# Values with the score as the stationary operand in the first two units, and transposes into x

## The chip, the cores and the metric

The kernel runs on one core of a Trainium2 chip. A core has five engines that work side by side, each through its own queue in the order of the program: TensorE (PE) multiplies matrices, VectorE (DVE) and GpSimd (POOL) do elementwise work, ScalarE (ACT) does functions and copies, and SyncE (SP) issues transfers (DMAs) here. They wait for each other by semaphores. TensorE reads its operands from SBUF, the large on-chip memory of 128 partitions, and writes only into PSUM, a small memory from which VectorE and ScalarE copy results away. GpSimd does not work on PSUM in this kernel. The metric is the time of one execution on the device in microseconds (us).

## The reference, cut to what matters

```python
# r, k, v, w: (4, 8, 768, 48); u: (8, 48)
for t in range(S):
    cur = einsum('bhd,bhe->bhde', u * k[t], v[t])
    y[t] = einsum('bhd,bhde->bhe', r[t], state + cur)
    state = w[t][..., None] * state + einsum('bhd,bhe->bhde', k[t], v[t])
x = y.transpose(0, 2, 1, 3).reshape(B * S, H * D)     # (3072, 384)
h = x @ moe_w_in                                      # (384, 2048)
out = (h / (1 + exp(-h))) @ moe_w_out                 # (2048, 384)
```

An attention with a decaying state, and behind it a network of two matrices with SiLU between them. All inputs and the output are float32.

## The kernel before, in words

**Units.** The work is cut into 12 units, each of 128 tokens (L = 128) of two of the four batches (b = 0 and 1). Of a unit, the attention gives x, 384 channels by 256 tokens; `up` (8 steps of 12 matmuls and a SiLU on ScalarE, L987 and L996) gives h; `down`, or `quarter` in later units, gives the output rows.

**Scores.** Within a unit a token sees the earlier ones through a matrix of scores, 128 keys by 128 queries for each batch and head, with the keys in partitions. The tile `score` holds all of it in two halves: e = 0 the even heads and e = 1 the odd ones; the heads of one half are counted by p = 0 to 3, so head h is 2p + e. Seven levels fill it (`scores`, levels 0 to 6, for blocks of 1 to 64 tokens): matmuls into a bank of PSUM (L704, L712), then per half either a masked copy by VectorE (`keep_masked`, L722) or two to four plain copies of blocks by ScalarE (L741). The list COPIED (L686) names the (unit, level, half) that ScalarE copies. `bonus_write` (L604, VectorE) writes the diagonal part with u; it reads it in unit 0 from p_w, a part of PSUM that the weights use too. Between the levels keys grow by products on GpSimd (L645, L669) and odd ones are copied by ScalarE (L615, L659), and queries grow by products on VectorE (L627).

**y in the first two units.** The units 0 and 1 have no earlier state to add. `y` (L859) takes, for each batch and head, the values as stationary operand (64 columns: the head's 48 and 16 beyond it, which is why the rooms of the values are 16 columns longer and set to zero there) and the scores as moving operand (128 columns). The output has channels in partitions: even heads from 0, odd heads from 64, so two matmuls lie in two halves of the array's columns. ScalarE copies the result of each batch to yt (L869).

**x in the first two units.** The channels of yt stand at 0 and 64, those of x have to stand without gaps. `dense_x` (L897) moves them with six matmuls per batch by matrices of ones, `dense`, which `clear_dense` (GpSimd, L303) and `make_dense` (ten copies by ScalarE, L317) build at the start. Of the four results ScalarE copies three to xt, and VectorE the second of unit 0 (L905). Later units use `y_state`, `y_values` and transfers instead (`move_x`), which the change leaves alone.

**Weights.** The kernel prepares the network's weights itself, while the first units run: 16 pieces, each loaded by a DMA into a staging place (L206, some of them only once an older piece has left the place) and split and joined again: `head_weight` (ScalarE, L223 and L225), `tail_weight` (ScalarE, L231, into p_w), `join_weight` (VectorE, L242 and L243, out of p_w), `add_weight` (GpSimd, L255). p_w holds one piece: L231 of the next waits for L243 of the one before. `up` waits for pieces 0 to 7, `down` for 8 to 15.

**The order** is written out by hand, in lists of steps given to `do` (from L1094); each engine gets its instructions in the order of these lists. Around the change in unit 0:

```python
do((bonus, 1, 0), (bonus, 1, 1), (bonus, 1, 2), *both(y, 0), (turn_apart, 0), (join_weight, 0), (add_weight,),
   (product, 1, 0), (tail_weight, 1), (turn, 1, 0, "k"), (join_weight, 1), (dense_x, 0, 0), (turn, 1, 1, "k"),
   (dense_x, 0, 1), (grow_queries, 1, 0), (odd_ones, 1), (tail_weight, 2), (turn_k, 0), (head_weight, 2), ...
   (up, 0, 0), ...
```

and in unit 1 (L1127): `(scores, 1, 6)`, steps of piece 8 and of unit 2, `(up, 0, 7)`, y, `(turn_apart, 1)`, `(tail_weight, 9)`, `(turn_k, 1)`, dense_x of b = 0, the first half of `head_weight` 9, dense_x of b = 1, its second half, `join_weight` 9, `tail_weight` 10, `head_weight` 10, `update` (L879 and L895), `(up, 1, 0)`. `turn_apart` (L820) is 16 small matmul records on TensorE and `turn_k` (L828) two copies of their results on ScalarE; `turn` of k is two copies for each b (L394, L395). `beat` (L1088) are transposes without use of their result.

Of the kernel before, what the change touches and what calls it, by code (L numbers as in the profile page):

```python
# [8 lines left out]
F32 = mybir.dt.float32  # L9
# [29 lines left out]
def kernel(  # L39
# [11 lines left out]
    nc = tc.nc  # L51
# [32 lines left out]
    def bank(name, *dims):  # L84

        have = banks[name][turns_of[name] % 2][:]
        turns_of[name] += 1
        steps, n = [], 1
        for d in dims[::-1]:
            steps.insert(0, [n, d])  # L90
            n *= d
        return bass.AP(tensor=have.tensor, offset=have.offset, ap=[have.ap[0], *steps])
# [33 lines left out]
    def load_values(i):  # L126
        n, b0 = units[i]
        t0 = n * L

        rooms = [pin.tile([128, H * D + PD - D], F32, name=name, bufs=2) for name in ("vt", "vq")]  # L130
        if n == 0:
            for room in rooms:
                nc.vector.memset(room[:, H * D:], 0.0)
        whole[i] = rooms
        vt[i], vq[i] = (room[:, 0:H * D].rearrange("p (h d) -> p h d", h=H) for room in rooms)
        nc.sync.dma_start(out=vt[i], in_=v[b0, :, t0:t0 + L, :].rearrange("h t d -> t h d"))
        if i < NTOK:
            nc.sync.dma_start(out=vq[i], in_=v[b0 + 1, :, t0:t0 + L, :].rearrange("h t d -> t h d"))
            return

        for g in range(4):
            t1 = t0 + L - (g + 1) * 32
            nc.sync.dma_start(out=vq[i][g * 32:(g + 1) * 32], in_=v[b0 + 1, :, t1:t1 + 32, :].rearrange("h t d -> t h d"))
# [152 lines left out]

    parts = sorted({(ch // 128, ch // (2 * D)) for ch in range(DM)})
    assert len(parts) == KC * 2

    dense = pt.tile([128, H, 2, D], F32, name="ruk", bufs=1).rearrange("p h s d -> p (h s d)").rearrange("p (x t) -> p x t", t=128)  # L300

    def clear_dense():
        nc.gpsimd.memset(dense, 0.0)  # L303

# [5 lines left out]

    def make_dense():
        for x, (c, p) in enumerate(parts):
            for e in range(2):
                at, rows = (2 * p + e) * D, slice(PD * e, PD * e + D)
                d0, d1 = max(0, c * 128 - at), min(D, (c + 1) * 128 - at)
                if d0 < d1:
                    nc.scalar.copy(out=dense[rows, x, at + d0 - c * 128:at + d1 - c * 128],  # L317
                                   in_=ident[rows, PD * e + d0:PD * e + d1])

# [366 lines left out]
    COPIED = (0, 5, 0), (0, 6, 0), (1, 6, 0)  # L686
# [172 lines left out]
    def y(i, b):  # L859

        p_yt[i, b] = ps.tile([128, NP, L], F32, name="p_h", bufs=2) if i == 0 else bank("p_m", NP, L)
        for p in range(NP):
            for e in range(2):
                h = 2 * p + e
                nc.tensor.matmul(p_yt[i, b][PD * e:PD * e + PD, p, :], lhsT=whole[i][b][:, h * D:h * D + PD],
                                 rhs=score[:, i % NSC, e, b * NP + p, :], start=(p == 0), stop=(p == NP - 1))
        if b == 0:
            yt[i] = pt.tile([128, NP, NB, L], F32, name="yt", bufs=1)
        nc.scalar.copy(out=yt[i][:, :, b, :], in_=p_yt[i, b])  # L869
# [27 lines left out]
    def dense_x(i, b):  # L897

        if b == 0:
            xt[i] = pt.tile([128, KC, TU], F32, name="xt", bufs=1)  # L900
        p_x = ps.tile([128, KC, L], F32, name="p_h", bufs=2) if i == 0 else bank("p_m", KC, L)
        for x, (c, p) in enumerate(parts):
            nc.tensor.matmul(p_x[:, c, :], lhsT=dense[:, x, :], rhs=yt[i][:, p, b, :],
                             start=(x == 0), stop=(x == len(parts) - 1))
        (nc.vector.tensor_copy if (i, b) == (0, 1) else nc.scalar.copy)(out=xt[i][:, :, b * L:(b + 1) * L], in_=p_x)  # L905
# [174 lines left out]
    def do(*steps):  # L1080
        for fn, *args in steps:
            fn(*args)
# [7 lines left out]
    def back(fn, i, *args):  # L1090
        return both(fn, i, *args)[::-1]
# [3 lines left out]
       (bonus_sum, 0, 0), (clear_dense,), (clear_state,), *back(turn, 0, "w"), (bonus, 0, 2), (bonus_sum, 0, 1), (start_keys, 0, nc.vector, True),  # L1095
       (start_keys, 0, nc.vector, False), (grow_queries, 0, 0), (product, 0, 0, nc.vector), (odd_keys, 0, 1), (grow_keys, 0, 1),
       (make_dense,), (beat, 16))
# [5 lines left out]
    for l in range(1, NL):  # L1103
        do((scores, 0, l), *[(grow_keys, 0, l + 1)] * (l + 1 < NL), *others[l])

    do((bonus, 1, 0), (bonus, 1, 1), (bonus, 1, 2), *both(y, 0), (turn_apart, 0), (join_weight, 0), (add_weight,),
       (product, 1, 0), (tail_weight, 1), (turn, 1, 0, "k"), (join_weight, 1), (dense_x, 0, 0), (turn, 1, 1, "k"),
       (dense_x, 0, 1), (grow_queries, 1, 0), (odd_ones, 1), (tail_weight, 2), (turn_k, 0), (head_weight, 2),
# [13 lines left out]
    for m in range(1, 4):  # L1122
# [4 lines left out]
    do((scores, 1, NL - 1), (bonus, 2, 0), (bonus, 2, 1), (join_weight, 8), (add_weight,), (bonus_sum, 2, 0), (bonus, 2, 2), (up, 0, 7), *both(y, 1), (turn_apart, 1),  # L1127
       (tail_weight, 9), (turn_k, 1), (dense_x, 1, 0), (head_weight, 9, [0]), (dense_x, 1, 1), (head_weight, 9, [1]),
# [66 lines left out]
```

## Time and profile before

| | |
|---|---|
| median of 3 runs | 606.24 us (606.04 to 606.5) |
| the profiled execution | 607.39 us, of which the span of the profile is 605.6 |
| granted clock of TensorE | 1.0 |
| busy in 30 to 66 us (36 us) | TensorE 34.1, VectorE 31.6, ScalarE 31.6, GpSimd 30.4 |
| busy in 66 to 90 us (24 us) | TensorE 23.5, VectorE 18.6, ScalarE 19.3, GpSimd 18.7 |
| y of unit 0 and unit 1 on TensorE | from 29.41 and from 66.75 |
| x of unit 0 and unit 1 on TensorE | from 32.51 and from 69.27 |

In a line of the profile, L12 is line 12 of the kernel before. PE is a matmul, PEld a load of its stationary operand; a float32 matmul shows as two records of each, so that 16 matmuls are "x32". A line of the timeline begins with the start and the length in us; lengths of matmuls overlap, so the pace is the distance from start to start. Names such as p_h<-score,vt are the tile written and the tiles read. A bracket at the end of a line is the time in which the engine stood idle before it, and who ended that. A line of waits names the waiting and the awaited group, then the sum in us, the number of waits and the longest. The chain is followed backwards from the last instruction, at each step to what released it.

### The profile page before, as it was taken

The page shows a single profiled execution, that of the slowest core. Times are in us where ns is not written, and L with a number is a line of the kernel's source. Part 1 is how long each engine was busy: PE and PEld are TensorE (multiplying, and loading weights), DVE is VectorE, ACT ScalarE, POOL GpSimd, SP SyncE. Part 2 cuts the span into 40 slices and gives each one's busy share as a digit, 9 for nine tenths or more (in the row PEclk, how much of TensorE's full clock was granted, in tenths as well). Part 3 has the DMA queues.
Part 4 walks back from the last instruction along what each step waited for, and adds up shares of the span by engine and source line. Part 5 has one row for each costly group of instructions (what it writes and reads, how often), then busy time and mean ns, then how long its engine had stood idle before and what let it go on. Part 6 is the DMA issues. An engine that isn't in the chain of part 4 may idle for free.

```text
span 605.6 us, 15147 instructions
## 1 busy us (share of the span) xinstructions
PE 593.4 (98%) x5982; PEld 529.5 (87%) x5982; DVE 416.8 (69%) x709; ACT 233.2 (39%) x516; POOL 366.6 (61%) x414
## 2 busy tenths in 40 slices
PE   8999999999998999999999999999999999999997
PEld 7787876799888899888889889889889989989997
DVE  7879779798795695696696687587587587451041
ACT  6788874431520530440351351351252242241110
POOL 6998777357578578378478478478568558500000
PEclk9999999999999999999999999999999999999999
DMA  9966693343532543643642643543553441100000
GB/s 224 312 148 168 124 307 47 56 77 49 127 70 48 106 65 52 137 61 56 130 65 50 130 62 53 121 69 52 115 83 53 98 70 27 36 2 27 28 1 26
DMA packets 203079, 53.44 MB, mean 88 GB/s; under 512 B 186752, under 2 KB 194816, under 8 KB 203008
## 3 DMA queue, kind: packets, MB, share of 16 engines
q1 hardware_dynamic: 201424, 51.88, 42.0%
q8 instruction: 47, 0.77, 0.6%
q10 hardware_dynamic: 1584, 0.59, 0.5%
q14 instruction: 24, 0.20, 0.1%
HBM read 43.21 MB, written 5.24 MB: 80 GB/s over the span
## 4 chain that ended last, share of the span: by engine, by line
PE 75%; DVE 8%; DMA 5%; POOL 3%; ACT 3%; SPq 2%; issue 2%; DVEq 0%; POOLq 0%; ACTq 0%
PE p_h L987 31%; PE p_o L1053 31%; PE p_m L1009 3%; PE p_m L852 2%; PE p_sc L704 2%; DMA tokens_w<-in_w_dram 2%; POOL tk L645 2%; DVE temps L1035 2%; PE p_m L704 1%; SPq L123 1%; PE p_m L844 1%; DVE score L722 1%; DVE tr L627 1%; DMA u_bc<-in_u_dram 1%; DVE p_w L242 1%
## 5 line engine op out<-in xcount | busy, mean ns | idle before, releaser
L987 PE MATMUL p_h<-xt,w_in_sb 128*128 128x256 f32 x1152 | 259.0, 382 | 0.9 <-POOL tk L669 0.7
L987 PEld LDWEIGHTS p_h<-xt,w_in_sb 128*128 128x128 f32 x1152 | 215.8, 190 | 32.1 <-POOL tk L669 0.9
L996 ACT ACTIVATE gt<-p_h 128x512 f32<-128x512 f32 x90 | 53.6, 597 | 189.4 <-PE p_h L987 189.1
L645 POOL TENSOR_TENSOR tk<-tk,tw 128x256 f32<-128x256 f32 x128 | 91.2, 734 | 42.8 <-issue 22.9
L1053 PE MATMUL p_o<-own,temps 128*128 128x192 f32 x528 | 88.7, 327 | 3.8 <-DVE temps L1062 3.8
L1053 PEld LDWEIGHTS p_o<-own,temps 128*128 128x128 f32 x528 | 86.0, 190 | 4.7 <-DVE temps L1062 4.6
L1053 PE MATMUL p_o<-w_out_sb,gt 128*128 128x192 f32 x508 | 87.4, 328 | 0.0
L1053 PEld LDWEIGHTS p_o<-w_out_sb,gt 128*128 128x128 f32 x508 | 82.7, 190 | 0.9 <-issue 0.4
L507 POOL TENSOR_TENSOR ruk<-tokens_rk 128x768 f32<-128x768 f32 (+1 forms) x32 | 51.3, 1613 | 49.6 <-DMA tokens_rk<-in_k_dram 25.5
L1035 DVE TENSOR_TENSOR temps<-gt 128x256 f32<-128x256 f32 x84 | 55.8, 664 | 22.4 <-ACT gt L996 22.4
L627 DVE TENSOR_TENSOR tr<-tr,tw 128x512 f32<-128x512 f32 x61 | 56.4, 925 | 18.2 <-PE p_m L704 14.4
L422 POOL TENSOR_TENSOR tw<-tw 128x256 f32<-128x256 f32 (+6 forms) x83 | 43.1, 519 | 37.1 <-DVE tw L374 33.2
L615 ACT COPY tk<-tk 128x256 f32<-128x256 f32 x52 | 21.0, 404 | 97.0 <-POOL tk L645 70.1
L1062 DVE TENSOR_TENSOR partial<-p_o,partial 128x192 f32<-128x192 f32 x33 | 11.8, 358 | 38.3 <-PE p_o L1053 38.1
L722 DVE COPY_PREDICATED score<-mask,p_sc 128x512 f32<-128x512 int8 x42 | 31.2, 798 | 3.1 <-PE p_sc L704 2.9
L1035 DVE TENSOR_TENSOR temps<-temps,gt 128x256 f32<-128x256 f32 x43 | 32.2, 748 | 1.5
L1053 PE MATMUL p_o<-w_out_sb,temps 128*128 128x192 f32 x176 | 30.4, 326 | 0.0
L1062 DVE TENSOR_TENSOR temps<-p_o,partial 128x192 f32<-128x192 f32 x22 | 7.9, 357 | 32.7 <-PE p_o L1053 23.3
L507 POOL TENSOR_TENSOR spare<-tokens_rk 128x384 f32<-128x384 f32 (+1 forms) x16 | 29.3, 1833 | 0.0
L857 ACT COPY yt<-p_m 48x512 f32<-48x512 f32 x40 | 23.2, 581 | 14.9 <-PE p_m L852 10.1
L1053 PEld LDWEIGHTS p_o<-w_out_sb,temps 128*128 128x128 f32 x176 | 28.9, 190 | 0.0
L704 PEld LDWEIGHTS p_sc<-tr,tk 48*32 48x32 f32 (+1 forms) x1312 | 18.2, 119 | 11.3 <-issue 6.8
(187 smaller groups left out, 840.5 us busy)
## 6 DMA issues: line engine op xcount, KB each, us to landing
w_out_sb<-in_moe_w_in_dram SPq DMA_DIRECT2D x6, 768.0 KB, 7.4
w_out_sb<-in_moe_w_out_dram SPq DMA_DIRECT2D x4, 768.0 KB, 5.8
own<-in_moe_w_out_dram SPq DMA_DIRECT2D x4, 768.0 KB, 6.2
tokens_rk<-in_r_dram SPq DMA_DIRECT2D x8, 384.0 KB, 4.4
tokens_rk<-in_k_dram SPq DMA_DIRECT2D x8, 384.0 KB, 5.4
tokens_w<-in_w_dram SPq DMA_DIRECT2D x8, 384.0 KB, 6.4
xt<-yt SPq DMA_DIRECT2D x60, 48.0 KB, 2.0
raw<-in_w_dram SPq DMA_DIRECT2D x80, 32.0 KB, 2.0
```

Source lines behind the costliest of these rows:

```text
L422: engine.tensor_tensor(out=up, in0=t[:, :, 0::2], in1=t[:, :, 1::2], op=ALU.mult)
L507: mul = lambda out, one, two: nc.gpsimd.tensor_tensor(out=out, in0=one, in1=two, op=ALU.mult)
L615: nc.scalar.copy(out=keys(i, X[(l + 1) % 2] * L + c, [4 * c, blocks], [c, 2], [1, c]), in_=keys(i, NP * L + c, [4 * c, blocks], [NP * L + ...
L627: nc.vector.tensor_tensor(out=odd, in0=odd, in1=tw[i][l][:, :, 0::2][:, :, :, None].to_broadcast([128, Q, L >> (l + 1), c]), op=ALU.mult)
L645: nc.gpsimd.tensor_tensor(out=out, in0=have, in1=odd_products(i, l, b, *blocks), op=ALU.mult)
L704: nc.tensor.matmul(to, lhsT=tk[i][rows, X[l % 2] + p, x * m:(x + 1) * m], rhs=have, start=True, stop=True)
L722: nc.vector.copy_predicated(out=dst, mask=masks[l][:, :, None].to_broadcast([128, NB, NP, ni, c]), data=sc[e].rearrange("p (b q) (i c) -> ...
L857: nc.scalar.copy(out=yt[i][PD * e:PD * e + D, :, b, :], in_=p_yt[i, e][PD * b:PD * b + D])
L987: nc.tensor.matmul(p_h[:, a, :], lhsT=w_in_sb[:, c, f * 128:(f + 1) * 128], rhs=xt[i][:, c, :], start=(c == 0), stop=(c == KC - 1))
L996: nc.scalar.activation(out=gt[i, m], in_=p_h, func=AF.Silu)
L1035: nc.vector.tensor_tensor(out=out, in0=one, in1=two, op=op)
L1053: nc.tensor.matmul(p, lhsT=left(f), rhs=right[:, f, :], start=(f == 0), stop=(f == FH - 1))
```

## The change

In units 0 and 1, `y` takes the scores as stationary operand (128 columns) and the values as moving operand (48 columns). The output has tokens in partitions and the 384 channels side by side without gaps, one bank for each batch. The matmuls go through both batches of the half e = 0 first, then of e = 1; one ScalarE copy of 384 columns per batch follows. `turn_x` then makes x by three transposes of 128x128 for each batch. The matrix of ones, its making and clearing, and the 16 zero columns of the values go. COPIED has one entry more: ScalarE, not VectorE, copies half e = 1 of the last level of unit 0. The steps keep their places in the lists, but for the two calls of y that become one.

```diff
-        rooms = [pin.tile([128, H * D + PD - D], F32, name=name, bufs=2) for name in ("vt", "vq")]
-        if n == 0:
-            for room in rooms:
-                nc.vector.memset(room[:, H * D:], 0.0)
+        rooms = [pin.tile([128, H * D], F32, name=name, bufs=2) for name in ("vt", "vq")]
...
-    def clear_dense():
-        nc.gpsimd.memset(dense, 0.0)
-    def make_dense():
...
-    COPIED = (0, 5, 0), (0, 6, 0), (1, 6, 0)
+    COPIED = (0, 5, 0), (0, 6, 0), (0, 6, 1), (1, 6, 0)
...
-    def y(i, b):
-        p_yt[i, b] = ps.tile([128, NP, L], F32, name="p_h", bufs=2) if i == 0 else bank("p_m", NP, L)
-        for p in range(NP):
-            for e in range(2):
-                h = 2 * p + e
-                nc.tensor.matmul(p_yt[i, b][PD * e:PD * e + PD, p, :], lhsT=whole[i][b][:, h * D:h * D + PD],
-                                 rhs=score[:, i % NSC, e, b * NP + p, :], start=(p == 0), stop=(p == NP - 1))
-        if b == 0:
-            yt[i] = pt.tile([128, NP, NB, L], F32, name="yt", bufs=1)
-        nc.scalar.copy(out=yt[i][:, :, b, :], in_=p_yt[i, b])
+    def y(i):
+        p_y = [ps.tile([128, H * D], F32, name="p_h", bufs=2) if i == 0 else bank("p_m", H * D) for b in range(NB)]
+        for e in range(2):
+            for b in range(NB):
+                for p in range(NP):
+                    h = 2 * p + e
+                    nc.tensor.matmul(p_y[b][:, h * D:(h + 1) * D], lhsT=score[:, i % NSC, e, b * NP + p, :], rhs=values(i, b)[:, h, :],
+                                     start=(e == 0 and p == 0), stop=(e == 1 and p == NP - 1))
+        yt[i] = pt.tile([128, NP, NB, L], F32, name="yt", bufs=1)
+        for b in range(NB):
+            y_rows[i, b] = yt[i].rearrange("p q b t -> p (q b t)")[:, b * H * D:(b + 1) * H * D]
+            nc.scalar.copy(out=y_rows[i, b], in_=p_y[b])
...
-    def dense_x(i, b):
+    def turn_x(i, b):
...
-        for x, (c, p) in enumerate(parts):
-            nc.tensor.matmul(p_x[:, c, :], lhsT=dense[:, x, :], rhs=yt[i][:, p, b, :],
-                             start=(x == 0), stop=(x == len(parts) - 1))
+        for c in range(KC):
+            nc.tensor.transpose(p_x[:, c, :], y_rows[i, b][:, c * 128:(c + 1) * 128], ident)
         (nc.vector.tensor_copy if (i, b) == (0, 1) else nc.scalar.copy)(out=xt[i][:, :, b * L:(b + 1) * L], in_=p_x)
```

## The prediction

> **What bounds the kernel now.** I read the page first, for shares of busy time and the chain.
>
> ```profile
> PE 593.4 (98%) x5982; PEld 529.5 (87%) x5982; DVE 416.8 (69%) x709; ACT 233.2 (39%) x516; POOL 366.6 (61%) x414
> PE 75%; DVE 8%; DMA 5%; POOL 3%; ACT 3%; SPq 2%; issue 2%; DVEq 0%; POOLq 0%; ACTq 0%
> ```
>
> TensorE is the bound of the whole, but a quarter of the chain runs elsewhere. The waits of TensorE from 90 us on show that little of that is late:
>
> ```profile
> PE p_o L1053 <- DVE temps L1062: 3.8, 2, 2.4
> ```
>
> These two waits hang by their chains on scores that TensorE itself finished, so they move with it. A shift of TensorE at 90 us therefore reaches the end whole, and the change lies wholly before 90. There I took the chain in order of time:
>
> ```profile
> 29.99 1.96 PE p_h L865 x30
> 31.95 0.63 PE p_sc L820 x16
> 32.58 1.55 PE p_h L903 x12
> 34.15 0.48 ACT xt L905
> ...
> 39.81 0.78 ACT p_w L231
> 40.61 0.97 DVE p_w L242
> ...
> 63.96 2.86 PE p_h L987 x12
> ```
>
> The reader is to see that unit 0's y and x (L865, L903) stand on the chain, and that after them it runs not through the matmuls of up but through the rounding of weights (ScalarE L231, VectorE L242, GpSimd L255), which feeds `up` at 63.96. In the timeline ScalarE is gapless from 34.15 to L231 at 39.71, and VectorE from L242 at 40.61 to 60.37. So what is late on ScalarE at 34.15 is late on TensorE at 63.96. Last, the timeline at both places of the change:
>
> ```profile
> 31.99 0.59 ACT L869 COPY yt<-p_h 128x512 f32<-128x512 f32 x1 [0.29 <-PE p_h L865]
> 32.47 0.88 ACT L231 ACTIVATE p_w<-w_out_sb 128x768 f32<-128x768 uint16 x1
> 34.15 0.48 ACT L905 COPY xt<-p_h 128x384 f32<-128x384 f32 x1 [0.19 <-PE p_h L903]
> ...
> 68.76 0.59 ACT L869 COPY yt<-p_m 128x512 f32<-128x512 f32 x1 [0.28 <-PE p_m L865]
> 69.25 0.89 ACT L231 ACTIVATE p_w<-w_out_sb 128x768 f32<-128x768 uint16 x1
> 72.26 0.48 ACT L905 COPY xt<-p_m 128x384 f32<-128x384 f32 x1
> 73.00 5.45 PE L987 MATMUL p_h<-xt,w_in_sb 128*128 128x256 f32 x24
> ...
> 89.34 0.70 PE L704 MATMUL p_sc<-tr,tk 48*64 48x64 f32 x32 [0.55 <-POOL tk L669]
> ```
>
> Right behind each second copy of y stands L231, the tail of the next weight: that is what y delays. 0.55 us is the only slack of TensorE between 72 and 121.
>
> [...] here are the loads.
>
> ```profile
> 25.07 0.97 PEld L590 LDWEIGHTS p_w<-own_sums,partial 128*128 128x128 f32 x8
> 32.51 2.75 PEld L903 LDWEIGHTS p_h<-yt,ruk 128*128 128x128 f32 x24
> 66.75 0.85 PEld L865 LDWEIGHTS p_m<-score,vt 128*64 128x64 f32 x16 [0.33 <-issue]
> 11.09 1.97 PE L1088 MATMUL p_m<-ident 128*128 128x128 f32 x16
> ```
>
> A row's length less one instruction (0.19 for a load of 128 columns), over the gaps: L903 (2.75-0.19)/23 = 0.111 us from record to record, and L590, whose moving operand has only 16 columns, (0.97-0.19)/7 = 0.111 too. So full 128-column weights set the pace, not the moving width. L865 with 64 columns in two column tiles runs at 0.05. [...] in a row they come (1.97-0.27)/15 = 0.113 apart, and each is one record, where every matmul here is two.
>
> **The change part by part, on TensorE.** y before: 32 records, 66.75 to 68.47 = 1.72 us (unit 0: 1.96 with its 0.34 wait for L722). After: 16 matmuls, 32 records, each with 128 columns of score as weights and 48 moving columns: 32 x 0.111 = 3.55. x before: 12 matmuls, 24 records, 2.75 per unit; after: 6 x 0.113 = 0.68. Per unit: +1.83 - 2.07 = -0.24 us of TensorE. That alone would be a gain of 0.5 us over both units; but it is in the wrong order: y, which others wait for, gets longer, and x, behind which something else is late, gets shorter. 48 moving columns lie between L590's 16 and L903's 128, so the pace is bounded by two equal rows.
>
> **Unit 0.** The third copied score tile goes from VectorE (L722, 0.74) to ScalarE, two copies, 0.70 of its queue. They must follow L604's write of the same tile (ends 29.09), end at 29.9, and delay L231 of weight 0 from 29.13 to 29.83; L242 and L243 of weight 0 follow 0.7 later and end at 32.7 instead of 32.0. VectorE idles 1.39 before the next L242, GpSimd 1.31 before L255: covered; uncovered it would be 0.7. No matmul waits for the copies: y now takes the half e=1 last, from about 31.3, so the 0.34 wait goes. y starts at 29.5 (29.41, plus 0.1 for leaving column tiles, which is what L590 to L386 shows: 0.22 against 0.11). Its last record starts at 29.5 + 31 x 0.111 = 32.94, takes 0.265 (L590 0.263, L903 0.275), and ScalarE begins the second y copy 0.03 later: 33.24, not 31.99. That copy is now 128x384: 0.48 as L905, not 0.59; so L231 of weight 1 comes at 33.63 instead of 32.47, +1.16. The four copies of k follow with it, and then L905, which waited 0.19 (0.24 by the queue's own pace) for L903 and now waits for nothing, since three transposes end at 34.4: it starts at 35.07, **+0.92**. What stands behind in ScalarE's queue (k, L659, L231, L828, L223, L225) goes 0.92 later without a gap. On VectorE, L242 of weight 1 waits for L231: 34.55; L243; then the second x copy at 36.5 instead of 35.49; `up` 0 starts at 37.1 instead of 36.2, a wait where TensorE has no cover, but its own lateness is no more than the pipeline's. GpSimd has part of this as slack (L255 of weight 1 at 36.6, +0.5). L242 at 40.61 becomes 41.5, VectorE has no gap until 60.4, and `up` at 63.96 comes 0.92 late.
>
> **Unit 1** (times without that 0.92). [...] first matmul 66.77, last 66.77 + 31 x 0.111 = 70.21, second copy of y at 70.50 instead of 68.76, L231 of weight 9 at 70.88 instead of 69.25, +1.63. Then, at the queue's pace as before, L828 to 72.54, first x copy 72.55, L223, second x copy 73.79 to 74.27. TensorE: transposes done by 71.5, the state's matmuls L879 wait for L828 until 72.57 (72.15 before), and `up` 1 waits for the second x copy until 74.3 instead of 73.0: **+1.30**. From there TensorE was gapless up to 88.79, where it waited **0.55** for GpSimd's L669. That chain is late too, but less: VectorE's 1.07 wait before L895 and ScalarE's 0.82 before L223 at 80.91 (for a weight's DMA) take up some. That DMA, issued at 76.32, does not move: SP's queue is gapless from 27.4 to 77 with loads of tokens, and what the DMA waits for, L243 of weight 9, ends at 74.7 (0.92 counted in). L669 ends near 90.8, TensorE arrives at 88.79 + 0.92 + 1.30 = 91.0.
>
> **Set to nothing.** The ten copies of the dense matrix (ScalarE, 13.0 to 15.1): ScalarE waited 0.79 behind them for L645. The clearing of it (GpSimd, 0.73 at 8.6): GpSimd waited 2.93 later. The four small memsets: VectorE then waited 1.29 for a load. If those covers were gone, each could give its own length, at most 2.1. No DMA is added or moved.
>
> **The sum**: 0.92 + 1.30 - 0.55 = +1.67 us on a span of 605.6, whose execution took 607.39 with what lies around it, 1.15 more than the median. I add the difference to the median: 606.24 + 1.67 = 607.9.
>
> **Rivals.**
> *Absorbed*: unit 0's delay is lost before 64, for instance because L722 and L242 get shorter [...] (one L722 pair took 2.48, others 1.30). Then 1.30 - 0.55 = +0.75, 607.0. Against it: VectorE has no gap from 40.6 to 60.4.
> *More*: GpSimd, not TensorE, releases L704 (90.8 against 91.0 is close), the 1.63 of L231 of weight 9 goes through to it whole, and the shifted queues collide for another 0.5 (the size of L255's spread below): 0.92 + 1.63 + 0.5 = +3.0, 609.2. For it: L255 took 2.29 at 36.12 and 1.84 elsewhere.
> *Not slower*: loads of score overlap better than L903's. It decides at 0.085 us a record: then `up` 1 is 0.5 late, which the 0.55 covers, and L905 of unit 0 is 0.1 late. At 0.056, twice the pace, unit 0 is held by the 0.7 on L231 of weight 0 (p_w is free at 32.7), and unit 1 by the same copies as before: 606.2, no gain. Against it: two rows at 0.111.
>
> **How the numbers follow.** Main case 0.55 (own range 607.4 to 608.6), Absorbed 0.20, More 0.15, Not slower 0.10. A difference under 0.2% (1.2 us, to 607.45) is about what a measurement cannot tell from none. Slower: 0.50 of the main case and More, 0.65; same: Absorbed, a little of the main case, most of Not slower, 0.29; faster 0.06, for starting work that I set to nothing. Range 606.6 to 609.3: it leaves out most of Not slower and the ends of the others.
>
> **What would show it.** In the profile after: y of 32 records 3.5 to 3.6 long in both units; six transposes about 0.11 apart; L231 behind y near 33.6 and 71.8; `up` 0 near 37.1, `up` 1 near 75.2; L704 of unit 2 near 91.0; after that the same gaps as before. The prediction is wrong if y's records come under 0.085 apart, or if `up` at 63.96 has not moved.

## The result and the profile after

The kernel after takes 609.38 us (median of 9 executions, 606.81 to 611.43), the kernel before 606.24 (median of 9). The ratio is 1.006, with a 95% interval from 1.0041 to 1.008: slower by 2.5 to 4.8 us. The profiled execution after took 609.52 us, its span is 607.7. The prediction had the direction right. The number was 1.5 us too low, and the time lies just above the end of the range.

The shares of the page, as of before: TensorE's busy time went up by 2.1 us, though the change took 36 records away from it (5982 to 5946), and the chain runs on it for 84% in place of 75%.

```profile
PE 595.5 (98%) x5946; PEld 531.6 (87%) x5946; DVE 418.4 (69%) x704; ACT 230.5 (38%) x508; POOL 364.8 (60%) x413
PE 84%; DVE 5%; DMA 3%; POOL 2%; SPq 2%; ACT 2%; issue 1%; DVEq 0%; POOLq 0%
```

In the kernel after, y is L845, its copies L850, the transposes into x L884 and their copies L885, `up` L967, `turn_apart` L797, the tail of a weight L227, its join L238 and L239. This is the timeline of TensorE around unit 0 (start, length, shapes, count, and in brackets the idle time before):

```profile
30.10 1.09 PE L845 MATMUL p_h<-vt,score 128*128 128x48 f32 x8
...
32.82 1.06 PE L845 MATMUL p_h<-vq,score 128*128 128x48 f32 x8
33.80 0.87 PE L797 MATMUL p_sc<-ident,tk 48*128 48x48 f32 x16
34.60 1.54 PE L884 MATMUL p_h<-ident,yt 128*128 128x128 f32 x6
37.77 4.41 PE L967 MATMUL p_h<-xt,w_in_sb 128*128 128x256 f32 x12 [1.62 <-DVE xt L885]
42.10 0.70 PE L681 MATMUL p_sc<-tr,tk 48*64 48x64 f32 x32
```

The y records follow each other as priced (eight of them 1.06 long). But the six transposes take 1.54 us, where unit 1's take 0.88. And `up` 0 takes 4.41 us, where the same 12 records took 2.83 before:

```profile
36.20 2.83 PE L987 MATMUL p_h<-xt,w_in_sb 128*128 128x256 f32 x12 [0.74 <-POOL tk L669]
```

The table of windows of the kernel after says why: its columns are the stretch, its length, the busy time of PE, PEld, DVE, ACT and POOL (in brackets their instructions), the granted clock, the DMA share and the GB/s moved.

```profile
30.10:33.80 3.70, 3.70 (x34) 3.65 (x32) 1.92 (x2) 1.57 (x3) 1.66 (x2) 1.00 0.35 52
34.20:41.00 6.80, 5.18 (x24) 4.07 (x21) 5.66 (x6) 6.46 (x13) 6.63 (x7) 0.50 0.45 58
42.10:45.50 3.40, 3.40 (x46) 3.02 (x46) 1.79 (x2) 3.26 (x5) 3.33 (x4) 1.00 1.02 382
```

The records of the clock put TensorE at half its clock from 34.14 to 40.97 us. In both profiles the stretches of one clock in these records, but for the last one at the end of the span, are whole multiples of 3.413 us: the 6.827 at half are two, the 27.307 of full clock ahead of them eight, the 566.612 behind them 166, and the 600.746 of full clock in the profile of before 176. One such piece is called a window of the clock below. The clock fell 0.3 us behind the end of y, among the 16 small transposes of L797 and ahead of any wait. No step of the prediction had that.

The queues, in the timeline of all engines, did what the prediction said:

```profile
33.91 0.48 ACT L850 COPY yt<-p_h 128x384 f32<-128x384 f32 x1 [0.41 <-PE p_h L845]
34.28 0.88 ACT L227 ACTIVATE p_w<-w_out_sb 128x768 f32<-128x768 uint16 x1
...
35.20 0.96 DVE L238 SCALAR_TENSOR_TENSOR p_w<-w_out_sb,p_w 128x768 uint32<-128x768 uint32 x1 [2.03 <-ACT p_w L227]
...
35.63 0.49 ACT L885 COPY xt<-p_h 128x384 f32<-128x384 f32 x1
...
37.07 0.55 DVE L885 COPY xt<-p_h 128x384 f32<-128x384 f32 x1
```

The second copy of x, for which `up` 0 waits, stands on VectorE behind the two halves of weight 1's join (from 35.20 and 36.20), and that join behind the tail at 34.28, and that behind y's second copy. In unit 1 the same timeline shows:

```profile
73.47 0.48 ACT L850 COPY yt<-p_m 128x384 f32<-128x384 f32 x1 [0.42 <-PE p_m L845]
...
73.85 0.90 ACT L227 ACTIVATE p_w<-w_out_sb 128x768 f32<-128x768 uint16 x1
...
74.00 0.88 PE L884 MATMUL p_m<-ident,yt 128*128 128x128 f32 x6
...
75.40 0.50 ACT L885 COPY xt<-p_m 128x384 f32<-128x384 f32 x1
75.77 0.95 ACT L219 ACTIVATE temps<-w_out_sb 128x768 bf16<-128x768 bf16 x1
...
75.96 0.56 PE L860 MATMUL p_m<-vt,kq 128*48 128x48 f32 x16 [1.09 <-ACT xt L885]
...
76.59 0.51 ACT L885 COPY xt<-p_m 128x384 f32<-128x384 f32 x1
```

Here the transposes end at 74.9, but their copies stand behind a tail, two copies of keys and half a head of the weights; `up` of unit 1 starts at 77.15.

**Two things to take off before comparing.** First, the start. The first product of level 1 of unit 0 comes at 13.81, in the profile of before at 13.31. That is no effect of the change: it goes with the moment at which TensorE's clock is first full in its records, 6.84 against 4.96 us (of 16 equal transposes, those from 1.36 us on took 3.68 in both profiles, those from 11.09 and 11.92 on 1.97). In a kernel that is the kernel before up to 86 us (the first experiment below) they were 13.79 and 6.91, in others 13.04 to 13.05 with 4.3 to 4.9. Over all profiles of this study the moment lay between 4.10 and 7.35 us; what sets it is not shown. All shifts below are therefore counted from that first product. Second, the end. In the profile of before the wait near 183 us was 2.38; in all other profiles of this study, late or not, it is 1.0 to 1.7. So that execution of before was about 1.2 us long in itself (it took 607.39, its median is 606.24), and spans are not compared.

Counted so, in the profiles of before and after: `up` 0 starts 1.06 later; it is 1.58 longer; `up` at 64 us starts 2.61 later; unit 1 adds 1.03; the 0.55 of slack near 90 us is used up; the first product of `quarter` (near 125 us) comes 3.02 later. The medians differ by 3.14.

### The profile page after: what moved, and what is told of

It is laid out like the page before. It is cut to its first block, busy times and chain, and to the rows that moved or that the text cites. A ratio compares the mean times of both kernels' runs of the same rounds, so it can differ in the third digit from the quotient of the medians.

```text
span 607.7 us, 15061 instructions
## 1 busy us (share of the span) xinstructions
PE 595.5 (98%) x5946; PEld 531.6 (87%) x5946; DVE 418.4 (69%) x704; ACT 230.5 (38%) x508; POOL 364.8 (60%) x413
## 4 chain that ended last, share of the span: by engine, by line
PE 84%; DVE 5%; DMA 3%; POOL 2%; SPq 2%; ACT 2%; issue 1%; DVEq 0%; POOLq 0%
PE p_h L967 37%; PE p_o L1033 31%; PE p_m L989 3%; PE p_m L829 2%; PE p_sc L681 2%; PE p_m L363 2%; PE p_m L681 2%; DVE temps L1015 2%; SPq L123 2%; POOL tk L622 1%; PE p_m L821 1%; DMA tokens_w<-in_w_dram 1%; PE p_m L797 1%; DMA raw<-in_k_dram 1%; PE p_sc L860 1%
## 5 line engine op out<-in xcount | busy, mean ns | idle before, releaser
L967 PE MATMUL p_h<-xt,w_in_sb 128*128 128x256 f32 x1152 | 260.5, 384 | 2.0 <-DVE xt L885 1.6
L967 PEld LDWEIGHTS p_h<-xt,w_in_sb 128*128 128x128 f32 x1152 | 217.0, 191 | 33.7 <-POOL tk L646 2.0
L1015 DVE TENSOR_TENSOR temps<-gt 128x256 f32<-128x256 f32 x84 | 57.8, 688 | 22.4 <-ACT gt L976 22.4
L604 DVE TENSOR_TENSOR tr<-tr,tw 128x512 f32<-128x512 f32 x61 | 58.5, 959 | 18.4 <-PE p_m L681 14.6
L1042 DVE TENSOR_TENSOR partial<-p_o,partial 128x192 f32<-128x192 f32 x33 | 11.8, 357 | 37.6 <-PE p_o L1033 37.5
L1015 DVE TENSOR_TENSOR temps<-temps,gt 128x256 f32<-128x256 f32 x43 | 30.2, 703 | 1.5
L865 POOL TENSOR_TENSOR state<-state,tw 128x512 f32<-128x512 f32 x16 | 21.9, 1389 | 10.3 <-PE p_m L821 10.3
```

The source lines that it names most:

```text
L604: nc.vector.tensor_tensor(out=odd, in0=odd, in1=tw[i][l][:, :, 0::2][:, :, :, None].to_broadcast([128, Q, L >> (l + 1), c]), op=ALU.mult)
L865: nc.gpsimd.tensor_tensor(out=new, in0=new, in1=tw[i][NL][:, b * NP:(b + 1) * NP, :].to_broadcast([128, NP, 2 * PD]), op=ALU.mult)
L967: nc.tensor.matmul(p_h[:, a, :], lhsT=w_in_sb[:, c, f * 128:(f + 1) * 128], rhs=xt[i][:, c, :], start=(c == 0), stop=(c == KC - 1))
L1015: nc.vector.tensor_tensor(out=out, in0=one, in1=two, op=op)
```

## The experiments

Each row is one kernel: shifts in its profile against the profile of before, counted from level 1's first product, in us; where its clock was at half in the stretch of units 0 and 1; in how many of its executions the clock fell; the medians of its executions and of before on the same chip; the ratio with its 95% interval.

| kernel | up 0 | up at 64 | unit 1's up | quarter | half clock (us of the span) | fell in | this / before | ratio |
|---|---|---|---|---|---|---|---|---|
| after | +1.06 | +2.61 | +3.64 | +3.02 | 34.1 to 41.0 | 8 of 9 | 609.38 / 606.24 | 1.0060 [1.0041, 1.0080] |
| late work | -0.01 | -0.03 | -0.03 | +1.92 | none | 0 of 22 | 607.86 / 605.82 | 1.0025 [1.0012, 1.0039] |
| one copy entry | +0.04 | +0.17 | +0.16 | 0.00 | none | 4 of 12 | 606.79 / 605.82 | 1.0014 [0.9994, 1.0034] |
| unit 0 alone | +1.05 | +2.71 | +2.70 | +2.53 | 34.3 to 41.2 | 5 of 7 | 608.79 / 606.27 | 1.0048 [1.0031, 1.0066] |
| unit 1 alone | +0.01 | -0.03 | +1.14 | +1.61 | 72.7 to 76.2 | 16 of 22 | 607.32 / 606.27 | 1.0017 [1.0004, 1.0031] |
| wide y | +1.11 | +2.65 | +3.71 | +3.16 | 37.6 to 41.0 | 5 of 6 | 610.00 / 606.27 | 1.0064 [1.0050, 1.0079] |
| filled wait | +1.05 | +1.40 | +2.51 | +3.03 | 34.0 to 37.4, 75.0 to 78.4 | 3 of 8 | 608.21 / 606.27 | 1.0042 [1.0026, 1.0058] |
| wide and filled, unit 0 and 1 | +1.12 | +1.42 | +3.48 | +2.73 | none | 0 of 12 | 609.01 / 605.82 | 1.0051 [1.0036, 1.0067] |
| wide and filled, unit 0 | +1.10 | +1.41 | +2.47 | +1.87 | none | 1 of 22 | 608.22 / 606.70 | 1.0023 [1.0008, 1.0038] |
| y's copy on VectorE | +3.16 | +4.79 | +6.26 | +5.51 | 39.9 to 43.3 | 6 of 6 | 610.85 / 605.82 | 1.0081 [1.0058, 1.0105] |
| other order | +0.01 | +1.91 | +1.47 | +4.91 | 34.7 to 41.5 | 6 of 6 | 612.06 / 606.70 | 1.0078 [1.0050, 1.0107] |
| other order, wide | -0.62 | +1.31 | +0.90 | +4.34 | none | 0 of 6 | 610.79 / 606.70 | 1.0056 [1.0034, 1.0079] |
| unit 0, other order, wide | -0.61 | +1.29 | +1.28 | +1.12 | none | 0 of 14 | 607.52 / 606.70 | 1.0013 [0.9997, 1.0029] |
| unit 0, late copy | -0.64 | +1.10 | +1.09 | +1.06 | none | 2 of 14 | 607.90 / 606.40 | 1.0034 [1.0016, 1.0053] |
| both, late copy | -0.65 | +1.09 | +1.25 | +1.16 | none | 1 of 22 | 607.67 / 606.40 | 1.0026 [1.0014, 1.0038] |

"Fell in" counts the executions whose mean granted clock was 0.997 or lower: one window of 3.41 us at half, 1.7 us of 607, is 0.28% of the span. It tells that the clock fell, not where; the column before it has the profiled execution alone. In the kernel before it fell in 2 of 41, 3 of 30, 5 of 35 and 0 of 35 executions where its median is 605.82, 606.27, 606.70 and 606.40.

### Does a shift near 90 us reach the end whole?

Late work: the kernel before, with 12 more records of `up` in unit 1.

```diff
-            for c in range(KC):
+            for c in [*range(KC)] * (2 if (i, m) == (1, 3) else 1):
```

> The kernel before, with the six products of the fourth step of unit 1's up (it starts near 93 us) done twice: 12 more records of 0.227 us, about +2.7 us of TensorE work after every wait of units 0 and 1; the output stays right. Step of the prediction ('a shift at 90 us reaches the end whole'): the time is 606.3 + 2.7 = 609.0, and the waits near 183 and 277 us stay 2.4 and 1.4 long. Rival (these waits hang on transfers that keep their own pace, and give back what TensorE comes late): the wait near 183 us is at most 1.2 long, and the time is near 607.6.

The place was misjudged in the expectation: the extra records stand at 86.5, ahead of the wait at 89.34, not behind it. TensorE's timeline of this kernel:

```profile
86.49 5.34 PE L987 MATMUL p_h<-xt,w_in_sb 128*128 128x256 f32 x24
91.76 0.70 PE L704 MATMUL p_sc<-tr,tk 48*64 48x64 f32 x32
```

So they first use up the 0.55 (no wait stands before L704 any more), and 2.7 - 0.55 = 2.2 is left. Measured: 1.92 at 125 us in the profile, +2.04 in the medians. What arrives at 125 us reaches the end here. The waits after 90 us, in this kernel and then in the one with one copy entry (columns: waiting and awaited group, us in total, number, longest):

```profile
PE p_o L1053 <- DVE temps L1062: 2.7, 2, 1.4
```

```profile
PE p_o L1053 <- DVE temps L1062: 2.6, 2, 1.4
```

The second of these kernels is not late at all at 125 us, and yet has the short waits; the 3.8 of before were that one execution's. The rival "the waits give lateness back" falls.

### The entry of COPIED

```diff
-    COPIED = (0, 5, 0), (0, 6, 0), (1, 6, 0)
+    COPIED = (0, 5, 0), (0, 6, 0), (0, 6, 1), (1, 6, 0)
```

> The kernel before with only the added entry of the list COPIED (unit 0, level 6, second half goes through the copy and not the product in place). Theory: nothing, 606.3 within 0.5, up 0 starts at 36.2 +- 0.3, no fall of the clock, and the first level's products start at 13.0 to 13.3. Rival (this entry lengthens the queues ahead of y): y and up 0 start 0.3 or more later, time 606.8 or more.

It moves `up` 0 by 0.04 and the products at 125 us by 0.00. The median is 0.97 above before, with an interval that holds no change. In 4 of the 12 executions the clock fell; these took 608.31 to 609.00 us, and the median of the other eight is 605.97. The kernel before had a fall in 2 of 41 on that chip, and in the profile here TensorE waits 1.18 us ahead of `up` 0, where it waited 0.74; whether the entry brings the falls is not shown. At full clock the prediction's "covered" stands.

### Each unit alone

Of the kernel before, unit 0 alone (with the entry of COPIED) or unit 1 alone got the new y and x:

```diff
-    ... *both(y, 0), ... (dense_x, 0, 0), ... (dense_x, 0, 1), ...
+    ... (y_new, 0), ... (turn_x, 0, 0), ... (turn_x, 0, 1), ...
```

> Only unit 0 with the new y, transposes and the third copied score tile; unit 1 as before. Clock falls in unit 0 as in the changed kernel, mean 0.994. The prediction's step for unit 0 gives up of unit 0 0.92 later and 607.2 without a fall; with the fall 1.6 more, less what waits near 183 us give back: 607.5 to 608.5. If the loss were in unit 1 it would be 606.2.

> Unit 0 as before, only unit 1 with the new y and transposes (the matrix of ones is still made). The prediction's sum for unit 1: up of unit 1 1.30 later, less the 0.55 slack, 607.0 against 606.24. With what the changed kernel's trace shows, that 1.2 of 2.4 us of waiting near 183 us was given back: the same as before, 605.8 to 606.5. The clock stays at 1.0 if the fall belongs to unit 0 alone.

Unit 0 alone has the delay, the same two windows of half clock, and most of the loss. Unit 1 alone makes its `up` 1.14 late, and in its profile the clock fell there too, for one window from 72.7; it fell in 16 of its 22 executions, against 3 of 30 of before. So unit 1's new form can bring a fall as well, though only the profiled execution shows where it was. In the profile of the kernel after the clock held in unit 1.

### What lets the clock fall

Wide y: the values are moved twice per matmul, 96 columns in place of 48; the second copy goes to spare columns of the bank that nothing reads.

```diff
...
-                    nc.tensor.matmul(p_y[b][:, h * D:(h + 1) * D], lhsT=score[:, i % NSC, e, b * NP + p, :], rhs=values(i, b)[:, h, :],
-                                     start=(e == 0 and p == 0), stop=(e == 1 and p == NP - 1))
+                    nc.tensor.matmul(dims_of(p_y[b], h * D, [H * D - h * D, 2], [1, D]), lhsT=score[:, i % NSC, e, b * NP + p, :],
+                                     rhs=dims_of(values(i, b), h * D, [0, 2], [1, D]),
+                                     start=True, stop=True)
...
```

> The changed kernel, but each matmul of y moves 96 columns instead of 48: the head's values twice, the second copy into spare columns of the bank. Theory narrow (y's 48 moving columns at a pace of 0.111 us [...] lets its clock fall to half at 34.1 us): the pace stays at 0.111, since 128 weight columns set it, the clock stays at 1.0 in every run, and the time falls from 609.4 to about 606.8, that of the one run of the changed kernel with a full clock. Theory wait (the 1.6 us in which TensorE waits before the first up let the clock fall): no difference, mean clock 0.994, 609.4.

The pace of y is unchanged (1.06 per eight), and the windows of the clock lie as in the profile of the kernel after (first full clock at 6.84 us in both). The fall right behind y is gone, but there is one a window later, and 5 of 6 executions had a fall. The windows of this kernel:

```profile
34.20:37.50 3.30, 1.16 (x18) 0.86 (x14) 2.21 (x3) 3.27 (x9) 3.30 (x5) 1.00 0.38 47
37.60:40.90 3.30, 3.08 (x7) 2.53 (x8) 3.20 (x4) 3.16 (x5) 3.23 (x3) 0.50 0.45 56
```

In the stretch behind y TensorE is busy for 1.16 of 3.30 us: small transposes and a wait. After that the clock is at half just when `up` 0 begins, so nothing is won.

Filled wait: narrow y, but two products of 256 columns that nobody uses stand in the wait before `up` 0.

```diff
+    def fill(n):
+        p = bank("p_m", TU)
+        for x in range(n):
+            nc.tensor.matmul(p, lhsT=ident, rhs=score[:, 0, 0].rearrange("p q t -> p (q t)")[:, 0:TU], start=True, stop=True)
...
-       (turn_x, 0, 1), (grow_queries, 1, 0), ...
+       (turn_x, 0, 1), (fill, 2), (grow_queries, 1, 0), ...
```

> The changed kernel with two matmuls of 256 columns, results unused, in TensorE's wait between the transposes of unit 0 and the first up; about 1.0 us of the 1.6 is filled, what is left is as long as the wait of the kernel before. Theory wait: the clock stays at 1.0, about 606.8. Theory narrow: the clock still falls at the end of y, at 34.1 us, before the filling; it comes back at most one window earlier, mean clock 0.994 to 0.997, 608 to 609.5.

Now the first window falls (34.0 to 37.4), right behind the narrow y, but not the second; `up` 0 takes 2.83 again, and `up` at 64 us is 1.40 late in place of 2.61. In this profile the clock fell in unit 1 too. Over its executions it fell in 3 of 8 only; these are too few to see the clock in their times (median of the three 607.83, of the other five 608.51).

Both together, in two versions. In the first, unit 1 got its two unused products as well:

```diff
-       ... (load_rk, 3), (up, 1, 0), ...
+       ... (load_rk, 3), (fill, 2), (up, 1, 0), ...
```

> The kernel after, with y's products over 96 columns (the values twice, the second copy goes to spare columns) and two products of 256 columns that nobody uses in each of the two waits, before up 0 and before unit 1's up. Waits, copies and the order of the queues are those of the kernel after; only TensorE is kept at work. Theory that the clock's fall is a part of the loss: no window of half clock in units 0 and 1, up 0 takes 2.83 us and not 4.41, up 0 starts at 37.8 and unit 1's up at 75.9 or less, and the time is near 607.0 (609.4 less two windows of about 1.2). Rival (the fall of the clock is given back later, and the delay of the queues alone is what counts): the clock holds, and the time is still 609.0 to 609.8.

The clock held, and the time was still 609.01. That looked like the rival, but in unit 1 the wait is before the products of the state, and the unused ones stood behind it, so that they cost TensorE their 1.1 us. Without them:

> The kernel with wide products and filled waits, but without the two unused products in unit 1, where they stood behind the wait, not in it, and cost TensorE 1.1 us themselves. So unit 0 has wide y products and the filled wait before up 0, unit 1 wide y products alone. Theory (the delays of the queues are those of the prediction, +1.67 together, and the fall of the clock in unit 0 is the rest of the 3.1): the clock holds in unit 0, up 0 takes 2.83 us, unit 1's up starts 1.1 to 1.4 sooner than at 76.2, and the time is 1.5 to 1.9 above before: near 607.6. Rival (the clock has no part in it): 608.8 or more, as with both waits filled.

TensorE's timeline of this kernel:

```profile
34.65 0.88 PE L885 MATMUL p_h<-ident,yt 128*128 128x128 f32 x6
36.04 1.13 PE L1075 MATMUL p_m<-score,ident 128*128 128x256 f32 x4 [0.52 <-ACT tk L372]
37.99 2.83 PE L968 MATMUL p_h<-xt,w_in_sb 128*128 128x256 f32 x12 [0.82 <-DVE xt L886]
```

`up` 0 waits as long as ever (its shift is +1.10), but TensorE is at full clock. The clock fell in 8 of 9 executions of the kernel after, and in 1 of 22 of this one. The loss is 1.52 us (0.5 to 2.3 by the interval) in place of 3.14 (2.5 to 4.8). The prediction's own sum, which had no clock in it, was 1.67. In the profiles the clock makes 2.61 - 1.41 = 1.20 us at 64 us and 3.02 - 1.87 = 1.15 at 125 us. So between a third and a half of the loss was the clock.

The next two runs, which differ in y's products alone (their moving columns, and the start and stop that each wide one carries), show what part of this is the narrow y.

### Another order of the steps

In unit 0 both `turn_x` right behind the tail of weight 1; in unit 1 both right behind the tail of weight 9, the second copy to x on VectorE, and the first step of `up` ahead of the state's products.

```diff
-       (product, 1, 0), (tail_weight, 1), (turn, 1, 0, "k"), (join_weight, 1), (turn_x, 0, 0), (turn, 1, 1, "k"),
-       (turn_x, 0, 1), (grow_queries, 1, 0), ...
+       (product, 1, 0), (tail_weight, 1), (turn_x, 0, 0), (turn_x, 0, 1), (turn, 1, 0, "k"), (join_weight, 1), (turn, 1, 1, "k"),
+       (grow_queries, 1, 0), ...
...
-       (tail_weight, 9), (turn_k, 1), (turn_x, 1, 0), (head_weight, 9, [0]), (turn_x, 1, 1), (head_weight, 9, [1]),
-       ... *both(update, 1), (bonus_sum, 2, 1), (load_rk, 3), (up, 1, 0), ...
+       (tail_weight, 9), (turn_x, 1, 0), (turn_x, 1, 1), (turn_k, 1), (head_weight, 9, [0]), (head_weight, 9, [1]),
+       ... (up, 1, 0), *both(update, 1), (bonus_sum, 2, 1), (load_rk, 3), ...
```

> The kernel after with another order of its steps alone. Unit 0: both turn_x stand right behind the tail of weight 1, ahead of the copies of k and of the join of weight 1. Unit 1: both turn_x stand right behind the tail of weight 9, turn_k follows, the second copy to x is made by VectorE, and the first step of up stands ahead of the state's products. Theory (up 0 and unit 1's up wait only because the copies to x stand behind work for weights and keys): up 0 starts near 36.4 and not 37.8, unit 1's up 1.5 us or more sooner after its y than now, and the time falls by 1.2 to 2.2 against the kernel after, to 607.2 to 608.2; the clock may fall as in the kernel after. Rival (the rounding of weights, which comes 0.6 later by this order, is what TensorE waits for up to 64 us): up 0 comes sooner, but TensorE waits 0.5 or more for weights before one of the steps of up between 45 and 67 us, and the time is 609 or more.

> As the kernel with the other order, and with y's products over 96 columns. Theory (half clock comes from y's narrow products first, and then from the long wait behind them): there is at most one window of half clock in unit 0, in most executions none, and the time is that of the other order less 0.5 to 1.5: near 606.5. Rival (the clock's falls don't matter or are not caused by these): times as with the other order alone.

TensorE's timeline with narrow y, and then with wide y:

```profile
34.65 1.54 PE L884 MATMUL p_h<-ident,yt 128*128 128x128 f32 x6
36.94 5.07 PE L967 MATMUL p_h<-xt,w_in_sb 128*128 128x256 f32 x12 [0.74 <-DVE xt L885]
```

```profile
33.70 0.88 PE L885 MATMUL p_h<-ident,yt 128*128 128x128 f32 x6
35.32 2.83 PE L968 MATMUL p_h<-xt,w_in_sb 128*128 128x256 f32 x12 [0.74 <-POOL tw L399]
```

With narrow y the clock fell in 6 of 6 executions, with wide y in none of 6, at the same wait of 0.74 us. So in this order the width of y's products decides: narrow ones let it fall, wide ones with a short wait hold it. The times are 612.06 and 610.79.

Narrow products are not enough everywhere, though. In unit 1 of the kernel after, the same 32 ran at full clock, from here to 73.4:

```profile
69.77 0.99 PE L845 MATMUL p_m<-vt,score 128*128 128x48 f32 x8
```

In the profile of the other order with narrow y the clock was likewise at half from 34.7 to 41.5 us only, and full during y of unit 1. Why it held there is not shown.

Both kernels of the other order are slower than the kernel after. Their times are the rival's, but TensorE waits for weights and keys near 90 us, not between 45 and 67 as the rival had it. In the waits of the kernel with narrow y from 90 us on, beside the usual ones:

```profile
PE p_m L989 <- POOL w_out_sb L251: 1.7, 1, 1.7
PE p_sc L681 <- POOL tk L646: 1.0, 1, 1.0
```

Unit 0 alone, in this order and with wide y:

> Unit 0 alone in the new form, with the other order of its steps and y's products over 96 columns; unit 1 as in the kernel before. Theory: up 0 starts at or before 36.4, no fall of the clock in most executions, and nothing is lost in unit 1: 605.6 to 606.4, so not slower than before, and perhaps 0.4 faster. Rival (the later rounding of weights decides): up 0 is early, but up at 64 us is 0.5 or more late, and the time is 606.8 or more.

This tells most about unit 0. `up` 0 starts 0.61 sooner than before, the clock holds in all 14 executions, and `up` at 64 us is 1.29 later than before all the same. Its timeline (lines as in the kernel before, but `up` is L1013) shows where the time goes:

```profile
35.80 2.83 PE L1013 MATMUL p_h<-xt,w_in_sb 128*128 128x256 f32 x12 [0.74 <-POOL tw L422]
...
43.01 2.86 PE L1013 MATMUL p_h<-xt,w_in_sb 128*128 128x256 f32 x12 [0.27 <-POOL w_in_sb L255]
...
46.34 0.29 PE L704 MATMUL p_sc<-tr,tk 48*64 48x64 f32 x2 [0.47 <-DVE score L722]
...
47.40 0.69 PE L704 MATMUL p_sc<-tr,tk 48*64 48x64 f32 x30 [0.77 <-DVE score L722]
```

As the prediction had it, the way to 64 us does not run through `up` 0 but through the queues of ScalarE, VectorE and GpSimd. They feed the weights and the scores, and they are late. The time is 607.52 against 606.70, with an interval that holds no change and up to 0.29%.

### Taking weight 1 out of y's way

y's second copy to VectorE. In the first try it kept its place in the list (added to the kernel with both waits filled):

```diff
-            nc.scalar.copy(out=y_rows[i, b], in_=p_y[b][:, 0:H * D])
+            (nc.scalar.copy, nc.vector.tensor_copy)[b](out=y_rows[i, b], in_=p_y[b][:, 0:H * D])
```

> As the kernel with wide products and filled waits, and the second of y's two copies on VectorE in place of ScalarE, in both units, so that ScalarE's queue is free one copy (0.9 us) sooner. Theory of the prediction (the later weight copies on ScalarE hold up 0 and unit 1's up): up 0 starts at 37.0 or sooner and not 37.8, unit 1's up about as much sooner, and the time is 0.5 to 1.2 less than that of the kernel with filled waits, near 606.2. Rival (VectorE's weight copies then come as much later, or the waits near 183 and 277 us give it back): up 0 or the end moves by less than 0.3, time as there.

A miss in the other direction: the copy stands ahead of the join of weight 0 in VectorE's queue, waits there for the end of y, and the join comes at 34.42 and not at 31.22 as in the kernel after. `up` 0 is 3.16 late. In the second try the copy stands behind that join, and the second copy to x is on ScalarE:

```diff
-    ... (turn_apart, 0), (join_weight, 0), (add_weight,),
+    ... (turn_apart, 0), (join_weight, 0), (add_weight,), (copy_y, 0),
```

> Unit 0 alone in the new form, wide products and the other order, as in the run before it, but y's second copy goes to VectorE behind the join of weight 0, and the second copy to x to ScalarE. So the tail of weight 1 starts right behind the first copy of y (0.8 sooner) and its join on VectorE near 34.2 and not 35.6. Theory (the queue of the weights holds up everything up to 64 us): measured from the first product of level 1, up of 64 us comes 0.0 to 0.6 later than before, not 1.3, and the time is 0.7 to 1.3 less than with unit 0 in the other order: 606.0 to 606.8 where before has 606.3. Rival (the longer y and its copies on the way to the scores hold it up): still 1.0 to 1.4 later, time as there.

The join of weight 1 is now only 0.54 later than before (counted from level 1's first product), and `up` at 64 us is still 1.10 late: the rival's numbers. The timeline shows what is late next:

```profile
34.27 0.86 ACT L937 COPY xt<-p_h 128x384 f32<-128x384 f32 x2 [0.72 <-PE p_h L936]
...
35.01 0.41 ACT L394 COPY tk<-p_m 128x256 f32<-128x256 f32 x1
...
36.87 0.88 ACT L231 ACTIVATE p_w<-w_out_sb 128x768 f32<-128x768 uint16 x1
...
37.29 1.83 POOL L255 TENSOR_TENSOR w_in_sb<-temps 128x768 uint32<-128x768 uint32 x1
```

ScalarE waits for the transposes, which wait for y. The copies of k, the tail of weight 2 (36.87; at 35.80 before, where level 1 began 0.29 later) and GpSimd's queue follow. So the tail of weight 1 was only the first thing behind y. The longer y holds up ScalarE's queue in every order that was tried.

Last, both units; in unit 1 y's second copy on VectorE, and both copies to x ahead of the head of weight 9:

```diff
-    ... (y, 1), (turn_apart, 1), (tail_weight, 9), (turn_k, 1), (turn_x, 1, 0), (head_weight, 9, [0]), (turn_x, 1, 1), (head_weight, 9, [1]),
+    ... (y, 1), (turn_apart, 1), (copy_y, 1), (tail_weight, 9), (turn_k, 1), (turn_x, 1, 0), (turn_x, 1, 1), (head_weight, 9, [0]), (head_weight, 9, [1]),
```

> The kernel after with wide products, unit 0 as in the run with unit 0 alone, and in unit 1 y's second copy on VectorE and both copies to x ahead of the first half of the head of weight 9. Theory: unit 1's up starts 6.2 to 6.7 us after its y (6.25 before, 7.4 after), the clock holds in most executions, nothing is left of the loss but 0 to 0.6 us, and the time is 606.0 to 607.0. Rival (head and join of weight 9, which this delays, decide as in the run with both units in the other order): unit 1's up is early, TensorE waits 1 us or more for weights near 90 us, and the time is 608 or more.

Unit 1's `up` starts 6.52 us after its y (before 6.25, after 7.38), with no wait for weights. At 125 us this kernel stands at +1.16, the one with unit 0 alone at +1.06. So in unit 1 the delay was a matter of order, and nearly all of it can be had back; in unit 0 1.1 us stay. The time is 607.67 against 606.40, ratio 1.0026: less than the kernel after loses, but above the 606.0 to 607.0 that was expected, and no version here beats the kernel before.

## Why the prediction was right and wrong

**The step that failed** is in the costing of TensorE and of unit 0: "48 moving columns lie between L590's 16 and L903's 128, so the pace is bounded by two equal rows". The pace was right. But the step counts y's matmuls as work like any other, and the `up` behind them as 2.83 us; the sum had no term for TensorE's clock, which the profile of before showed full throughout. Narrow products for 3.6 us, then 16 small transposes, six larger ones and a wait, let the clock fall to half until 41 us, and `up` 0 ran in that. This took +1.58 us on `up` 0, and 1.20 of that arrived at 64 us (2.61 against 1.41 with the clock held), where the whole predicted sum was 1.67. The predicted wait before `up` 0 was priced at its length; what a wait does to the work behind it was not asked. The clock is in none of the rivals either. "More" had the right size of time (609.2) by luck: its first reason did not come (L704 near 90 us was not released later by GpSimd; its wait is gone), and the "another 0.5" of its second is near what unit 0 had beyond 0.92 at 64 us (0.49, below), but was taken from the spread of L255.

**Right, with sizes**, counted from level 1's first product where a time is meant:

- y: 32 records at 0.111 us predicted; eight of them measure 1.06 in both units, and 0.265 for the last from its start, so (1.06 - 0.265)/7 = 0.114.
- Transposes 0.113 apart predicted; (0.88 - 0.27)/5 = 0.12 in unit 1 at full clock.
- Unit 0: tail of weight 1 at 33.63 predicted, 34.28 - 0.50 = 33.78 measured; first copy of x 35.07 against 35.63 - 0.50 = 35.13; `up` 0 +0.92 against +1.06. At 64 us, with the clock held, it is +1.41, where the prediction carried 0.92 through: too small by 0.49, and where that arises was not traced.
- That this delay, and not `up` 0, sets what happens at 64 us: shown by unit 0 in the other order (`up` 0 at -0.61, `up` at 64 at +1.29). That it is the tail of weight 1 in particular is not so; the whole of ScalarE's queue is late.
- Unit 1: +1.30 against +1.03. Here the order of the waits was another: the products of the state waited not for the copies of keys, but for the first copy to x.
- The slack of 0.55 was used; what is late at 125 us reaches the end (late work: 1.92 at 125 us, +2.04 in the medians).
- The entry of COPIED moves nothing in a profile at full clock; whether it brings falls of the clock is open.

In the kernel that holds the clock (wide and filled, unit 0) the terms are 1.41 + 1.06 - 0.55 = 1.92; its profile stands at +1.87, and its median lost 1.52 (0.5 to 2.3). The predicted 1.67 fits these, in part by luck: unit 0 was put 0.49 too low at 64 us and unit 1 0.24 too high.

**Wrong in a detail**: "after that the same gaps as before". The wait near 183 us was 1.17 and not 2.38. The cause lies in the profile of before, not in the kernel after. The prediction noticed that its profiled execution was 1.15 above the median, and did not ask where. And L255 took 2.15 to 2.16 us at three other places (47.88, 52.98 and 56.74), not 1.84 everywhere but at 36.12; only a rival used that.

**Open.** The ten copies of the matrix of ones, its clearing and the memsets were not tried alone; no profile here shows a gain or a loss that is theirs. What TensorE's clock reacts to is not shown beyond this: behind y of unit 0, in the other order, 96 moving columns held it at the same pace (0 of 6 falls) and 48 did not (6 of 6). How much work keeps the clock full, why it fell in unit 1 in some profiles and not in others, and why the kernel with the one copy entry fell in 4 of 12 executions was not tried.

## What to carry to other kernels

Price a change on TensorE not only by its records times their pace, but also by how many columns each of them moves (in the other order 48 let the clock fall in 6 of 6 executions, 96 at the same pace in 0 of 6), and by what runs right behind: here 3.7 us of narrow products, small transposes and a wait of 1.62 went with half clock on the next large block, for +1.58 us on that block and +1.20 at 64 us. When a result comes late in an engine's queue, ask what stands behind it in that queue (here y's second copy at 33.91, and the tail of weight 1 behind it at 34.28), and then what stands behind that; moving the first thing out of the way only shows the second. And before a wait late in a profile is used in an argument, see whether it is the same in another execution.

## What the runs showed of the hardware

- Half clock came in windows of 3.41 us: one in the profiles of wide y (37.6 to 41.0) and of unit 1 alone (72.7 to 76.2), two together in that of the kernel after (34.14 to 40.97). There the clock fell right behind 3.7 us of narrow products without any gap (30.10 to 33.80, busy 3.70), and the longest wait near it, which came after the fall, was 1.62.
- The kernel before had a mean granted clock of 0.997 or lower in 10 of the 141 executions that were run beside the experiments, and those ten took 608.57 to 611.73 us, where the medians of before lie between 605.82 and 606.70. By the 3.41 us of a window and the 0.50 granted in it, the estimate of what one can cost TensorE is at most 1.7 us, and these ten lay 2.3 to 5.9 above the median of their chip; so something else was late in them too, and which came first is not shown.
- The moment of the first full clock moved by 3.25 us between profiles (4.10 to 7.35 us), and with it the start of level 1 (13.02 to 14.04), whatever the kernel.
